# Chunked retention with transposes by DMA, and a second matmul in seven products, in a fused retention and hard-swish MLP kernel

## The chip, the cores and the metric

The kernel runs on one core of a Trainium2 chip. The metric is the device time of one launch in microseconds. Each kernel was run several times; medians with their lowest and highest run are given. A run's own record also has its span (first to last instruction in the trace) and the mean clock that the tensor engine was granted, as a share of full speed.

The engines are named as the profile names them: PE is the tensor engine (PEld its weight loads), DVE the vector engine, ACT the scalar engine, POOL is GpSimd, SP is the engine that here only issues DMA. A `q` behind a name (ACTq, SPq) means the sequencer of that engine, for instance while it issues a DMA.

## The reference

```python
# q, k, v: (8 batches, 8 heads, 576 positions, 64), float32
scores = q @ k^T / sqrt(64)
gamma  = 1 - 2.0 ** (-5 - h)                        # one decay per head
ret    = scores * where(i >= j, gamma ** (i - j), 0)
x      = (ret @ v)  as (8 * 576 tokens, 8 * 64)      # 4608 x 512
h      = x @ w_in                                    # 512 -> 2048
g      = h * clip(h + 3, 0, 6) / 6
out    = g @ w_out                                   # 2048 -> 512, float32
```

## The kernel before

Both kernels compute in fp16 with fp32 sums in PSUM. The kernel before handles one batch (576 tokens) of retention at a time, two heads together. It loads q, k and v through GpSimd's casting DMA queue, transposes q and k on PE, computes all 576 x 576 scores of the causal half, multiplies them by a table of decays on DVE, and multiplies by v. Between these steps it emits units of the MLP for blocks of 512 tokens that are ready.

```python
for b in range(B):
    # ... token blocks whose batches are done are queued; pop_units(4)
    for c in range(H // 2):                          # two heads
        # ... cast_load of q, k, v on the gpsimd queue
        for nix, nat in enumerate((qn16, kn16)):
            pst = psum.tile([P, S], FP16, tag="pp")
            for j in range(NCH):                     # 5 chunks: 4 x 128 + 64
                nc.tensor.transpose(pst[:, P*j:P*j+sj], nat[0:sj, j, :], ident16[...])
            # copy to SBUF: q by vector, k by scalar
        pop_units(2)
        for grp in bgrp:                             # 4 groups of score columns
            # ... matmuls kt2 x qt2 into pms[0], pms[1]
            for h2 in range(2):
                nc.vector.tensor_tensor(out=at16s[h2][...], in0=pms[h2][...],
                                        in1=dmask[...], op=ALU.mult)     # L210
        pop_units(2)
        for (s0, s1) in m2sc:
            # ... matmuls vn16 x at16s, scalar.copy into xt16              # L230, L236

def moe_unit(kb, kind, ix):                          # block of 512 tokens
    if kind == 0:                                    # "up": one of 16
        for dmc in range(NCC):                       # 4 matmuls of 512 columns, L122
            nc.tensor.matmul(ph, win16[:, dmc, ...], xt16[:, dmc, tok0:tok0+MBLK], ...)
        nc.scalar.activation(u, ph, ACTF.Relu, bias=0.5, scale=1/6)         # L126
        nc.vector.scalar_tensor_tensor(out=gt16[:, fc, :], in0=u, scalar=1.0,
                                       in1=ph, op0=ALU.min, op1=ALU.mult)   # L128
    else:                                            # "down": one of 4
        for fc in range(NFC):                        # 16 matmuls of 512 columns, L136
            nc.tensor.matmul(pout, gt16[:, fc, P*mc:P*mc+P], wout16[:, fc, :], ...)
        # ... scalar.copy to osb, store
```

## Time and profile before

| | before |
|---|---|
| time, first three runs | 454.21 us median (450.7 to 455.75) |
| span of the profiled run | 448.7 us |
| PE busy | 394.0 us, 88% |
| first up-projection matmul | at 47.8 us |
| period of one batch in the middle | 48.4 us, PE busy 44.2 us of it |
| one block's up, one block's down, alone | 13.8 us each |

The first lines are from the profile's page: the span, the busy time of each engine, the busy share of the engine in 40 equal slices (a digit is tenths), the granted clock in the same slices, and the chain of waits, which is the path followed back from the last instruction.

```profile
span 448.7 us, 6207 instructions
...
PE 394.0 (88%) x2368; PEld 181.7 (40%) x2368; DVE 230.5 (51%) x432; ACT 201.6 (45%) x349; POOL 177.6 (40%) x222
...
PE   0387999989998999899998999899989999899996
...
PEclk9999999999998999999999999999998999999999
...
PE 69%; DVE 18%; ACT 9%; issue 2%; POOL 1%; DVEq 0%; POOLq 0%
```

PE is busy in nearly every slice, at or near full clock. The kernel is bound by PE with short interruptions. The next lines are the end of the chain of waits in order of time (start, duration, what), where nothing but the MLP runs.

```profile
390.36 13.06 PE ph L122 x60
403.41 13.81 PE pout L136 x64
417.23 13.81 PE ph L122 x64
431.04 13.83 PE pout L136 x64
```

This gives the price of the MLP: 64 matmuls of 512 columns take 13.81 us, or 216 ns each. A batch period in the middle holds one up and one down, 27.6 us, so the other 20.8 us of the 48.4 us go to retention and its waits. The table of windows shows such periods (start:end, length, then busy time of each engine).

```profile
98.40:146.80 48.40, 44.45 (x277) 20.40 (x275) 27.21 (x52) 21.04 (x39) 20.74 (x24) 0.96 0.70 63
146.80:195.20 48.40, 44.22 (x282) 20.73 (x281) 27.21 (x52) 21.73 (x40) 20.79 (x24) 1.00 0.70 63
195.20:243.60 48.40, 44.22 (x282) 20.75 (x281) 27.21 (x52) 21.72 (x40) 20.80 (x24) 1.00 0.70 63
```

### The profile page before, as it was taken

What the parts mean: (1) busy time and instruction counts of PE and PEld (TensorE: products, weight loads), DVE (VectorE), ACT (ScalarE), POOL (GpSimd) and SP (SyncE); (2) the same over time, 40 slices, a digit from 0 to 9 for tenths busy, and PEclk for the clock granted to TensorE, in tenths of its full rate; (3) what the DMA queues carried; (4) which work ended last, traced back from release to release, by engine and by line L of the source; (5) the groups of instructions that cost most, each with busy time, mean ns of one, the idle gap of its engine ahead of it and who ended that gap; (6) DMA issues with size and microseconds to landing.
All of it is one profiled execution on the core that took longest, in us unless ns stands there. A gap on an engine that the chain in (4) does not pass through costs nothing.

```text
span 448.7 us, 6207 instructions
## 1 busy us (share of the span) xinstructions
PE 394.0 (88%) x2368; PEld 181.7 (40%) x2368; DVE 230.5 (51%) x432; ACT 201.6 (45%) x349; POOL 177.6 (40%) x222
## 2 busy tenths in 40 slices
PE   0387999989998999899998999899989999899996
PEld 0133444434443444444443444344443444344442
DVE  0254675347716672467635771667245763480540
ACT  5623564156522663356415652266325641571641
POOL 9966799763534444155326353445200000000000
PEclk9999999999998999999999999999998999999999
DMA  5999999985777766487568568776210001001101
GB/s 36 123 189 192 120 96 96 154 75 37 46 92 88 46 45 61 86 55 50 37 101 74 39 44 93 87 50 42 39 70 1 0 1 70 26 0 48 47 23 70
DMA packets 134700, 29.73 MB, mean 66 GB/s; under 512 B 126480, under 2 KB 130064, under 8 KB 134672
## 3 DMA queue, kind: packets, MB, share of 16 engines
q0 software_dynamic: 129488, 19.91, 60.8%
q1 hardware_dynamic: 5184, 9.44, 5.7%
q8 instruction: 18, 0.29, 0.3%
q14 instruction: 10, 0.08, 0.1%
HBM read 39.80 MB, written 9.44 MB: 110 GB/s over the span
## 4 chain that ended last, share of the span: by engine, by line
PE 69%; DVE 18%; ACT 9%; issue 2%; POOL 1%; DVEq 0%; POOLq 0%
PE pout L136 28%; PE ph L122 22%; DVE at16a L210 8%; DVE at16b L210 6%; PE pst L174 5%; ACT dmask L80 3%; ACT xt_104 L236 2%; ACT u L126 2%; ACT sb L180 2%; DVE gt_6_3580 L128 1%; DVE gt_5_3055 L128 1%; DVE gt_0_430 L128 1%; DVE gt_4_2530 L128 1%; DVE gt_3_2005 L128 1%; DVE gt_2_1480 L128 1%
## 5 line engine op out<-in xcount | busy, mean ns | idle before, releaser
L122 PE MATMUL ph<-xt_104,win_102 128*128 128x512 f16 x576 | 143.2, 383 | 5.7 <-DVE gt_1_955 L128 0.8
L126 ACT ACTIVATE u<-ph,cb 128x512 f32<-128x512 f32 x144 | 97.2, 687 | 53.2 <-PE ph L122 51.0
L122 PEld LDWEIGHTS <-win_102 128*128 128x128 f16 x576 | 52.6, 97 | 71.0 <-issue 19.5
L140 ACT COPY osb<-pout 128x512 f32<-128x512 f32 x36 | 21.1, 585 | 111.5 <-PE pout L136 111.5
L178 DVE COPY sb<-pst 128x576 f16<-128x576 f16 x32 | 14.5, 455 | 43.3 <-PE pst L174 43.3
L200 PEld LDWEIGHTS <-sb 64*128 64x128 f16 (+1 forms) x384 | 14.9, 100 | 42.5 <-ACT sb L180 18.2
L180 ACT COPY sb<-pst 128x576 f16<-128x576 f16 x32 | 20.4, 637 | 3.6 <-PE pst L174 1.6
L128 DVE SCALAR_TENSOR_TENSOR gt_8_4320<-u,ph 128x512 f16<-128x512 f32 x16 | 11.0, 688 | 16.6 <-ACT u L126 16.6
L128 DVE SCALAR_TENSOR_TENSOR gt_6_3580<-u,ph 128x512 f16<-128x512 f32 x16 | 10.7, 681 | 9.0 <-ACT u L126 8.9
L128 DVE SCALAR_TENSOR_TENSOR gt_2_1480<-u,ph 128x512 f16<-128x512 f32 x16 | 10.5, 679 | 9.2 <-ACT u L126 9.2
L128 DVE SCALAR_TENSOR_TENSOR gt_5_3055<-u,ph 128x512 f16<-128x512 f32 x16 | 10.7, 681 | 8.0 <-ACT u L126 7.8
L128 DVE SCALAR_TENSOR_TENSOR gt_4_2530<-u,ph 128x512 f16<-128x512 f32 x16 | 10.7, 681 | 8.0 <-ACT u L126 7.8
L128 DVE SCALAR_TENSOR_TENSOR gt_0_430<-u,ph 128x512 f16<-128x512 f32 x16 | 10.5, 680 | 8.3 <-ACT u L126 8.3
L128 DVE SCALAR_TENSOR_TENSOR gt_1_955<-u,ph 128x512 f16<-128x512 f32 x16 | 10.5, 680 | 8.1 <-ACT u L126 8.1
L128 DVE SCALAR_TENSOR_TENSOR gt_3_2005<-u,ph 128x512 f16<-128x512 f32 x16 | 10.5, 680 | 8.1 <-ACT u L126 8.1
L136 PE MATMUL pout<-wout_103,gt_2_1480 128*128 128x512 f16 x64 | 14.3, 379 | 0.2 <-DVE at16a L210 0.2
L136 PE MATMUL pout<-wout_103,gt_4_2530 128*128 128x512 f16 x64 | 14.3, 379 | 0.2 <-DVE at16a L210 0.2
L136 PE MATMUL pout<-wout_103,gt_0_430 128*128 128x512 f16 x64 | 14.3, 379 | 0.2 <-DVE at16a L210 0.2
L136 PE MATMUL pout<-wout_103,gt_1_955 128*128 128x512 f16 x64 | 14.3, 379 | 0.2 <-DVE at16a L210 0.2
L136 PE MATMUL pout<-wout_103,gt_5_3055 128*128 128x512 f16 x64 | 14.3, 379 | 0.2 <-DVE at16a L210 0.2
L136 PE MATMUL pout<-wout_103,gt_6_3580 128*128 128x512 f16 x64 | 14.3, 379 | 0.2 <-DVE at16a L210 0.2
L136 PE MATMUL pout<-wout_103,gt_3_2005 128*128 128x512 f16 x64 | 14.3, 379 | 0.2 <-DVE at16a L210 0.2
(1059 smaller groups left out, 775.9 us busy)
## 6 DMA issues: line engine op xcount, KB each, us to landing
out_dram<-osb SPq DMA_DIRECT2D x36, 256.0 KB, 2.0
win_102<-in_moe_w_in_dram POOLq DMA_DIRECT2D x2, 640.0 KB, 8.8
wout_103<-in_moe_w_out_dram POOLq DMA_DIRECT2D x2, 640.0 KB, 10.0
win_102<-in_moe_w_in_dram POOLq DMA_DIRECT2D x1, 768.0 KB, 9.9
wout_103<-in_moe_w_out_dram POOLq DMA_DIRECT2D x1, 768.0 KB, 10.5
qn_108<-in_q_dram POOLq DMA_DIRECT2D x2, 80.0 KB, 3.0
kn_109<-in_k_dram POOLq DMA_DIRECT2D x2, 80.0 KB, 3.0
vn_110<-in_v_dram POOLq DMA_DIRECT2D x2, 80.0 KB, 3.1
```

What stands on the lines that cost most here:

```text
L80: nc.scalar.activation(dmask[:, h, :], rsel, ACTF.Exp, bias=cb[:, 1:2], scale=float(np.log(gamma[h])))
L122: nc.tensor.matmul(ph, win16[:, dmc, P * fc:P * fc + P], xt16[:, dmc, tok0:tok0 + MBLK], start=(dmc == 0), stop=(dmc == NCC - 1))
L126: nc.scalar.activation(u, ph, ACTF.Relu, bias=cb[:, 0:1], scale=1.0 / 6.0)
L128: nc.vector.scalar_tensor_tensor(out=gt16[:, fc, :], in0=u, scalar=1.0, in1=ph, op0=ALU.min, op1=ALU.mult)
L136: nc.tensor.matmul(pout, gt16[:, fc, P * mc:P * mc + P], wout16[:, fc, :], start=(fc == 0), stop=(fc == NFC - 1))
L140: nc.scalar.copy(osb, pout)
L174: nc.tensor.transpose(pst[:, P * j:P * j + sj], nat[0:sj, j, :], ident16[0:sj, 0:sj])
L178: nc.vector.tensor_copy(sb, pst)
L180: nc.scalar.copy(sb, pst)
L200: nc.tensor.matmul(pms[h2][0:mt, co:co + ns], kt2[base:base + D, P * tcix:P * tcix + mt], qt2[base:base + D, a:bb], start=True, stop=True)
L210: nc.vector.tensor_tensor(out=at16s[h2][0:mtg, alo:alo + wid], in0=pms[h2][0:mtg, 0:wid], in1=dmask[0:mtg, 2 * c + h2, alo:alo + wid], op= ...
L236: nc.scalar.copy(xt16[h2 * D:h2 * D + D, c, b * S + s0:b * S + s1], pos[h2][h2 * D:h2 * D + D, 0:s1 - s0])
```

## The change

The intent is to make retention linear in the length of the sequence and to take its transposes off PE.

- **Chunks.** A batch's 512 first positions are four chunks of 128. q is multiplied by gamma^(i-e) and k and v by gamma^((e-j)/2) each, so a chunk's scores need only a 0/1 mask, and the sum of k^T v stays in PSUM as a state without being decayed. A chunk takes 24 matmuls of 128 columns: 8 for the scores, 8 for the values, 4 with the state of earlier chunks, 4 that add to the state.
- **Tails.** The 64 last positions of two batches make one more chunk, and the tails of all eight batches form a ninth token block. There are 36 chunks.
- **Transposes by DMA.** q and k of a chunk (256 KB) are transposed from SBUF to SBUF by one DMA, issued by ACT.
- **Seven products.** The down-projection of eight blocks is done as a 2 x 2 block product with seven products of 16 matmuls of 256 columns; DVE builds the sums. It runs one block behind the up-projection.
- **Order by hand.** No scheduler moves instructions: each engine runs what it is given in the order of the program. The preparation of a chunk is `load` (three DMAs on SP, six for a tail), `cast` (three multiplications on GpSimd), `xpose` (the transpose, ACT). Its use is `ret1` (scores and mask) and, some matmul groups later, `ret2` (the rest). How far preparation runs ahead of use is set in `advance`, called at the end of each `ret2`.

```diff
-            for nix, nat in enumerate((qn16, kn16)):
-                ...
-                    nc.tensor.transpose(pst[:, P * j:P * j + sj],
-                                        nat[0:sj, j, :], ident16[0:sj, 0:sj])
+    def cast(c, engs):
+        ...     # qk16[q|k] = staged q, k times table; vpad = staged v times table
+    def xpose(c):
+        qk = qk16s[c]
+        qt = work.tile([P, 8, P], FP16, tag="qkT", bufs=4, name="qkT")
+        qkTs[c] = qt
+        nc.scalar.dma_start_transpose(qt, qk.rearrange("p a h d -> p (a h d)"))
+    def ret1(c):
+        ...     # sc = kT x qT, 8 matmuls (L140); at = sc * mask on vector (L147)
+    def ret2(c):
+        ...     # xp = v x at + state x qT (L162, L167); state += k x v (L184)
+        ...     # xt <- xp on scalar (L189), s16 <- state on scalar (L196)
+    ...
+    nxt = [4]
+    nxp = [5]
+    def advance(i):
+        while nxp[0] < NCHK and nxp[0] <= i + 2 and nxp[0] < ncast[0]:
+            xpose(order[nxp[0]])
+            nxp[0] += 1
+        if nload[0] < NCHK and nload[0] <= i + 7:
+            load(order[nload[0]])
+            nload[0] += 1
+        if ncast[0] < nload[0] and ncast[0] <= i + 3:
+            cast(order[ncast[0]], G3)
+            ncast[0] += 1
+    def r2():
+        if nxt[0] < NCHK:
+            ret2(order[nxt[0]])
+            advance(nxt[0])
+            nxt[0] += 1
+    xpose(order[5])          # six chunks are cast and transposed by here
+    nxp[0] = 6
+    ...                      # blocks 0 and 1: up() with r1(), r2() between
+    for mc in range(4):
+        r1()
+        down_plain(0, mc)    # 16 matmuls of 512 columns, L248
+        r2()
+        tbuild(mc)
+    for kb in range(2, 9):
+        ...                  # 16 up(kb, fc), with r1() at 2, 9 and r2() at 5, 12
+        product(pb, "P1")    # pb = kb - 1; 16 matmuls of 256 columns, L312
+        r1()
+        product(pb, "P6")
+        r2()
+        product(pb, "P2")
+        r1()
+        product(pb, "P7")
+        r2()
+        ...                  # P5, r1, P4, r2, P3
```

## The prediction

> **What bounds the kernel now.** The tensor engine, in program order. The page gives PE 88% busy of a 448.7 us span (VectorE 51%, ScalarE 45%, GpSimd 40%); the chain of waits is 69% PE, 18% VectorE, 9% ScalarE. In time it shows about 50 us before the first up-projection matmul, seven batch periods of 48.4 us, and 54.5 us of two token blocks alone. There one up-projection of a block (64 matmuls, 128x512) takes 13.8 us and one down-projection 13.8 us (216 ns a matmul). So a batch period is 27.7 us of MLP and about 20.7 us of retention, of which some 4 us per period is the chain sitting in the VectorE mask products (0.60 to 0.69 us each).
>
> **What the change does.**
> - Removes all PE transposes (0.82 us per head pair) with their PSUM copies, and the quadratic part: a head pair now streams 2x1600 columns twice. Chunked, a 128-token chunk of all heads needs 24 matmuls of 128 columns. Transposes in the trace start about 90 ns apart, and 64-row pairs start together, so I estimate 1.7 us a chunk, 7.7 us a batch (4.5 chunks) against 20.7.
> - Seven products of 16 matmuls of 256 columns replace 64 of 512 for eight blocks: 112 x about 110 ns = 12.3 us against 13.8 (estimate). Gain 12 us in all.
> - VectorE: mask work falls from about 16 us to 5.5 us a batch; the sums for the seven products and five PSUM additions add about 8.5 us. ScalarE: relu stays (16 x 0.69 us a block), plus 36 DMA transposes issued from it; nothing in this trace shows their issue time, I assume about 2 us each.
> - Input loads move from GpSimd's casting queue to SP, in the same 256-byte rows. GpSimd multiplies instead; the Trainium skill ("GPSIMD Engine Reference", Performance versus the Vector engine) has 4.5 us for a 2048-element two-input fp32 operation, so I estimate 1.1 us per 512 and 3.5 us a chunk, below the 7 us a chunk is due in.
> - DMA: the windows show the 16 queues full at about 110 GB/s written as fp16, i.e. 220 GB/s read, while q, k, v are loaded. 28.3 MB at that rate is 129 us, weights and output some 50 us, and the transposes (256 KB each) about 1 us each at the 261 GB/s of "DMA: Bandwidth & Descriptors", Latency and other measured facts. About 215 us of the span: not the bound, except in the first 60 us.
>
> **Sum (span).** Head until the first up-projection: 26 us (loads, casts, four serial chunks), plus 5 us waiting for loads of chunks six to eight. Then PE: nine up-projections 124, one plain down 14, eight seven-product downs 98, 32 chunks 54: 290 us. Small stalls 12 us (ScalarE and PE are nearly equal in the up stage, about 17.5 us each), tail 4 us. Together 337 us; before's timed runs exceed its profile span by 5.5 us. **Prediction 343 us, 8 in 10 between 312 and 388.** Faster by over 2%: 0.95; within: 0.03; slower: 0.02.
>
> **What would show it.** First up-projection matmul near 26 us; period of a block in the middle 34 to 37 us; product matmuls 110 ns apart; PE at or above 85% after the head; chain mostly PE; VectorE about 26 us and ScalarE below 30 us per block.
>
> **What would make it wrong.** DMA transposes that occupy ScalarE or the queues much longer than 2 us, delaying relu and so PE's four PSUM buffers; loads slower than 220 GB/s, so that chunks arrive late and PE waits (GpSimd multiplies would then wait on DMA); 128-column matmuls nearer 60 ns (about 15 us better).

## The result, and the profile after

| | before | after |
|---|---|---|
| time | 452.45 us median of 4 runs (450.3 to 455.8) | 431.12 us median of 4 runs (426.88 to 436.98) |
| span of the profiled run | 448.7 us | 431.8 us |
| PE busy | 394.0 us | 318.7 us |
| PE idle | 54.7 us | 113.1 us |
| mean granted clock | 0.991 | 0.919 |
| first up-projection matmul | 47.8 us | 35.15 us |

The ratio of the times is 0.9448, 95% interval 0.9349 to 0.9547. Ratios here are the mean time of one kernel's fast runs over that of the other's fast runs of the same rounds, so they are not quite the ratio of the medians. Two of the four runs after, the profiled one among them, are marked slow because they are over 1.5% above the fastest; the fast ones had clocks of 0.932 and 0.923, so the low clock is no property of the slow runs. Their median is 427.8 us, which is the number to compare other fast runs with. The first experiment below has a profile with the same picture.

The kernel became faster, but by 21 us by these medians (25 us by the ratio of the fast runs) where 111 us were predicted. PE lost 75 us of busy time and gained 58 us of idle time. The page of the kernel after:

```profile
span 431.8 us, 6156 instructions
...
PE 318.7 (74%) x2368; PEld 197.1 (46%) x2368; DVE 228.1 (53%) x323; ACT 154.3 (36%) x273; POOL 110.0 (25%) x115
...
PE   0435966618754488877896869786979999999983
...
PEclk9999986959668878999989899998799999999999
DMA  9999983499256639777957597779533102020123
...
q1 hardware_dynamic: 126336, 46.15, 52.5%
q10 hardware_dynamic: 38016, 9.44, 14.8%
...
PE 50%; DMA 36%; SPq 5%; DVE 4%; ACT 2%; issue 1%; POOL 1%; POOLq 0%; ACTq 0%
```

DMA has 36% of the chain of waits, yet after the first 60 us the DMA row is full in a few slices only. This suggests that the chain waits for the duration of single transfers more than for the capacity of the queues; the experiments below test it. The list of waits (engine, line and tile, what it waited for: us in total, times, longest) and the view of the tile `qkT`, the transposed chunk, name the transfer:

```profile
PE sc L140 <- DMA qkT<-qk: 94.8, 29, 12.6
...
L131 ACTq DMA_TRANSPOSE qkT<-qk x36: 1247/1302/2072, 6.4 to 335.8; - x36
...
DMA to landing us min/median/max: 3.0/4.9/10.8
```

For 29 of 36 chunks, PE stood idle until the transpose of exactly this chunk had landed, for 94.8 of its 113.1 idle us (12.6 us of them for the very first chunk, 77.7 us after the first up-projection). Issuing one costs ACT's sequencer 1.3 us (median), and it lands 4.9 us after issue (median). The chain in order of time, in the stretch of the plain down-projection of block 0:

```profile
117.47 6.16 DMA qkT<-qk
...
123.67 0.61 PE sc L140 x8
124.28 6.07 PE po L248 x16
...
131.35 6.11 DMA qkT<-qk
...
137.50 0.61 PE sc L140 x8
138.11 5.98 PE po L248 x16
```

This reads: a transpose is issued, PE waits 6 us for it, computes the scores, runs one down group; then the rest of the chunk, and only now is the next transpose issued. The same stretch as a timeline (start, duration, engine and line, what, and in brackets the idle time before with its end):

```profile
117.13 0.36 SPq L240 DMA_DIRECT2D out_dram<-osb  x1
117.19 0.60 ACT L189 ACTIVATE xt<-xp 128x512 f16<-128x512 f32 x1
117.47 1.56 ACTq L131 DMA_TRANSPOSE qkT<-qk  x1
...
123.67 0.61 PE L140 MATMUL sc<-qkT 64*128 64x128 f16 x8 [6.30 <-DMA qkT<-qk]
```

Putting together, for single chunks, the end of GpSimd's last multiplication that the transpose needs, its issue, its landing and its use (all from the trace, us) shows that the input was ready long before:

```
chunk   input ready   issued   landed   scores start   PE idle before
 11         97.2       117.5    123.6      123.7            6.3
 12        102.6       131.3    137.5      137.5            6.3
 13        110.5       144.9    150.6      150.6            5.6
 20        188.2       208.8    214.0      214.0            1.9
 24        221.9       243.2    250.3      250.3            2.9
 30        270.3       293.8    300.7      300.8            3.6
```

The input was ready about 18 to 34 us before the transpose was issued, for every chunk from 11 on. ACT was not busy with other work all this time (36% over the span); the instruction simply stands late in its program.

The program says why. `advance(i)` runs after `ret2(i)`. Its bound for transposes reads `nxp <= i + 2`, two chunks ahead. But a transpose also needs `nxp < ncast`, and `ncast` is 6 when the first call comes, with `i = 4`, and rises by one per call because the cast is an `if`, and it stands after the transposes. So `ncast` is always `i + 2` when the transposes are looked at, and only chunk `i + 1` passes, the one that the very next `ret1` needs. The text says two ahead, the program does one.

The waits also cost a second time. The windows (length, busy PE, PEld, DVE, ACT, POOL, clock, DMA share, GB/s) show the clock that PE was granted:

```profile
64.00:106.00 42.00, 23.54 (x139) 11.54 (x140) 16.67 (x24) 15.64 (x25) 12.47 (x12) 0.76 0.85 156
106.00:158.00 52.00, 30.68 (x160) 13.64 (x158) 14.32 (x19) 7.82 (x16) 12.75 (x12) 0.74 0.48 89
...
238.00:282.00 44.00, 34.89 (x303) 23.13 (x304) 25.46 (x35) 16.63 (x29) 18.27 (x16) 0.96 0.82 144
```

Where PE idles 5.6 to 6.3 us between groups the mean clock is 0.74, and a down group of 16 matmuls takes 6.0 to 6.3 us; the same group of the kernel before took 3.45 us. A mean over such a stretch hides what happens in it. Here is one down group by itself, and the wait after it:

```profile
122.80:129.20 6.40, 5.53 (x20) 2.15 (x21) 2.45 (x3) 0.00 (x0) 2.08 (x2) 0.50 0.17 22
129.40:136.20 6.80, 1.85 (x21) 1.20 (x19) 0.00 (x0) 1.80 (x4) 1.04 (x1) 1.00 0.72 155
```

The clock is 0.50 while the group runs and 1.00 while PE mostly waits: it follows the work with a delay, so that nearly all of the group runs at half clock. The Trainium skill ("TensorE: Matmul & The Clock Gate", Part 1: The HAM clock gate) says that PE's clock is halved after an idle window of about 3.4 us and restored after a busy one; the 0.50 behind gaps of about 6 us agrees with it. A block's period in the steady part is 42 to 43 us (the score matmuls of chunks 18, 23, 28 and 33 start at 195.8, 238.3, 281.4 and 324.5 us), where 34 to 37 us were predicted.

### The profile page after: what moved, and what is told of

It is laid out like the page before. It is cut to its first block, busy times and chain, and to the rows that moved or that the text cites. A ratio compares the mean times of both kernels' runs of the same rounds, so it can differ in the third digit from the quotient of the medians.

```text
span 431.8 us, 6156 instructions
## 1 busy us (share of the span) xinstructions
PE 318.7 (74%) x2368; PEld 197.1 (46%) x2368; DVE 228.1 (53%) x323; ACT 154.3 (36%) x273; POOL 110.0 (25%) x115
## 3 DMA queue, kind: packets, MB, share of 16 engines
q1 hardware_dynamic: 126336, 46.15, 52.5%
q10 hardware_dynamic: 38016, 9.44, 14.8%
HBM read 36.70 MB, written 9.44 MB: 107 GB/s over the span
## 4 chain that ended last, share of the span: by engine, by line
PE 50%; DMA 36%; SPq 5%; DVE 4%; ACT 2%; issue 1%; POOL 1%; POOLq 0%; ACTq 0%
DMA qkT<-qk 30%; PE ph L218 20%; PE accB L312 10%; PE po L248 6%; SPq L94 4%; PE accA L312 4%; PE accC L312 4%; DMA st<-in_v_dram 3%; PE xp L162 3%; PE sc L140 3%; DMA st<-in_q_dram 2%; DVE g L223 2%; DMA wst<-in_moe_w_in_dram 1%; PE xp L167 1%; DVE ss L276 1%
## 5 line engine op out<-in xcount | busy, mean ns | idle before, releaser
L221 ACT ACTIVATE u<-ph,half 128x512 f32<-128x512 f32 x144 | 96.3, 687 | 108.5 <-PE ph L218 90.4
L218 PE MATMUL ph<-xt,win 128*128 128x512 f16 x512 | 132.0, 414 | 2.1 <-ACT xt L189 1.6
L223 DVE SCALAR_TENSOR_TENSOR g<-u,ph 128x512 f16<-128x512 f32 x144 | 95.5, 684 | 64.6 <-ACT u L221 63.5
L218 PEld LDWEIGHTS <-win 128*128 128x128 f16 x576 | 57.7, 104 | 72.9 <-issue 20.4
L140 PE MATMUL sc<-qkT 64*128 64x128 f16 x288 | 17.0, 248 | 94.8 <-DMA qkT<-qk 94.8
L117 POOL TENSOR_TENSOR qk<-st,tq 128x512 f16<-128x512 f32 x32 | 35.5, 1110 | 180.1 <-DMA st<-in_q_dram 114.5
L147 DVE TENSOR_TENSOR at<-sc,mask 128x1024 f16<-128x1024 f32 x32 | 39.1, 1223 | 69.1 <-PE sc L140 69.1
L312 PEld LDWEIGHTS <-ss 128*128 128x128 f16 x512 | 49.0, 98 | 8.0 <-DVE ss L276 1.7
L121 POOL TENSOR_TENSOR vpad<-st,tkv 128x512 f16<-128x512 f32 x36 | 38.8, 1078 | 22.3 <-DMA st<-in_v_dram 20.4
L312 PEld LDWEIGHTS <-g 128*128 128x128 f16 x384 | 37.7, 100 | 6.9
L117 POOL TENSOR_TENSOR qk<-st,tkv 128x512 f16<-128x512 f32 x32 | 34.7, 1084 | 5.5 <-DMA st<-in_k_dram 5.0
L162 PEld LDWEIGHTS <-vpad 128*128 128x128 f16 x288 | 23.8, 105 | 15.5 <-issue 11.8
```

The lines of the kernel that those rows point to most:

```text
L117: engs[ix].tensor_tensor(out=qk[:, ix, :, :], in0=st[:, ix, :, :], in1=tab.unsqueeze(2).to_broadcast([P, H, D]), op=ALU.mult)
L121: engs[ix].tensor_tensor(out=vp[:, :, 0:4:3, :], in0=st[:, ix, :, :].rearrange("p (a z) d -> p a z d", z=2), in1=tab.rearrange("p (a z) -> ...
L140: nc.tensor.matmul(sc[:, z, p, :], qt[z * D:z * D + D, HP + p, :], qt[z * D:z * D + D, p, :], start=True, stop=True)
L147: nc.vector.tensor_tensor(out=at.rearrange("p z a i -> p (z a) i"), in0=sc.rearrange("p z a i -> p (z a) i"), in1=m[:, :].unsqueeze(1).to_ ...
L162: nc.tensor.matmul(xp[:, p, :], vp[:, p, 2 * z:2 * z + 2, :], at[:, z, p, :], start=first, stop=False, skip_group_check=True)
L218: nc.tensor.matmul(ph, win16[:, m, P * fc:P * fc + P], xt[:, m, :], start=(m == 0), stop=(m == NCC - 1))
```

## Experiments

Two theories stood at the start. **Order**: the transposes are issued one chunk ahead, so their latency is on PE's path. **Bandwidth**: the queues are loaded with small packets of q, k and v, so the transposes, which share them, land late whenever they are issued. A third candidate was the stall of SP: the loads of output weights wait for buffers from about 47 to 82 us, and the load of chunk 9 stands behind them, which gave the longest single wait in mid kernel, 12.4 us. All ratios below are against the kernel before, in the same rounds on the same chip.

### x1_loads_early

```diff
-        if nload[0] < NCHK and nload[0] <= i + 7:
+        while nload[0] < NCHK and nload[0] <= i + 7:
```

> Loads of later chunks are issued up to the seven that the rule allows instead of one per step, so that they stand ahead of the output-weight loads on SP; transposes stay one chunk ahead. Theory A (the changed kernel loses its time because each DMA transpose is issued only one chunk before its use, and ScalarE's queue holds it back although its input was ready some 20 us earlier): only the 12.4 us wait at chunk 9 and a little of the cold clock go; 410 to 425 us. Theory B (the DMA queues as a whole are the bound, loads and transposes together): no gain, 425 to 435 us. A theory that late loads, not late transposes, are the cause would give under 380 us.

Measured: 429.9 us median (425.86 to 430.72, four runs), ratio 0.9481 (0.9398 to 0.9565). PE's waits for transposes were 82.7 us in 27 waits, landing after 4.7 us (median), clock 0.922. The wait at chunk 9 shrank from 12.4 to 7.0 us, and the time stayed where it was: PE now waited 8.0 us for casts of output weights, for which it did not wait before. So the stall of SP is not the main cause. The time lies in the range expected under theory B, bandwidth (425 to 435 us), and outside that under theory A, order (410 to 425 us): a miss of the theory that x2 then bears out. This run shows the waits of the kernel after: 83.4 us of idle time after the first up-projection, 65.1 us of it waits for transposes.

### x2_ahead2

x1, and one word more:

```diff
-        if ncast[0] < nload[0] and ncast[0] <= i + 3:
+        while ncast[0] < nload[0] and ncast[0] <= i + 3:
```

Now `ncast` can reach `i + 4` in `advance(i)`, and the bound `i + 2` of the transposes takes effect. With this word alone, without that of x1, the build stops with a deadlock, so that kernel was not run; the reading, not traced, is that a cast then waits for a load that SP, in order, cannot reach. That is why x1 is the base, and why x1 was measured by itself.

> As x1_loads_early, and multiplies are emitted while they may, so that each transpose is issued two chunks ahead instead of one. Theory A: the wait of the score matmuls for the transposed tile falls from 95 us to below 35 us (what is left is in the head), the granted clock rises from 0.92 to above 0.96, time 350 to 375 us. Theory B (DMA queues are the bound): that wait stays above 65 us and the time above 400 us.

Measured: 364.28 us (363.62 to 366.01, four runs), ratio 0.8055 (0.7993 to 0.8118). One word took away 65.6 us against x1. It makes the casts earlier too, but in x1 as in the kernel after the input of every chunk from 11 on lay ready over 17 us before the issue, so it acts through the earlier issue. The granted clock came out at 0.959 to 0.966, about the 0.96 expected. The waits for transposes and their landing, from the list of waits and the tile view of x2_ahead2:

```profile
PE sc L140 <- DMA qkT<-qk: 27.5, 7, 12.6
...
DMA to landing us min/median/max: 3.0/5.8/10.0
```

A transpose took longer to land than in the kernel after (5.8 against 4.9 us), while the same DMA traffic fell into less time. Yet the waits fell from 94.8 to 27.5 us, and in the trace none is left after chunk 13. Chunk 20, for example, was issued at 161.3, landed at 167.4 and was used at 172.7 us. The windows of x2_ahead2 show three blocks' periods in a row:

```profile
178.00:211.00 33.00, 32.92 (x295) 22.05 (x293) 24.65 (x35) 17.23 (x32) 18.11 (x17) 1.00 1.10 195
211.00:244.00 33.00, 32.41 (x292) 21.54 (x291) 24.70 (x35) 16.39 (x29) 14.61 (x14) 1.00 0.84 147
244.00:277.00 33.00, 32.96 (x296) 22.09 (x295) 25.60 (x38) 16.94 (x30) 6.90 (x6) 1.00 0.29 65
```

PE is full at full clock, and a block takes 33.0 us, slightly less than the 34 to 37 us predicted. The chain in order of time in the first of these windows gives the prices of the new work:

```profile
184.94 0.22 PE state L184 x4
185.16 1.75 PE accA L312 x16
186.91 0.33 PE sc L140 x8
187.24 1.85 PE accB L312 x16
```

A product of 16 matmuls takes 1.75 to 1.85 us, and a chunk takes 0.33 us for its scores, about 0.67 us for values and state terms and 0.22 us to add to the state, 1.22 us in all, or 51 ns a matmul.

### x3_ahead3

x1, with the bounds one further:

```diff
-        while nxp[0] < NCHK and nxp[0] <= i + 2 and nxp[0] < ncast[0]:
+        while nxp[0] < NCHK and nxp[0] <= i + 3 and nxp[0] < ncast[0]:
-        if ncast[0] < nload[0] and ncast[0] <= i + 3:
+        while ncast[0] < nload[0] and ncast[0] <= i + 4:
```

> As x2_ahead2 with transposes three chunks ahead. Theory A: a transpose lands 3 to 9 us after issue and a step of a chunk takes 5 to 9 us, so two ahead hides nearly all; three ahead gives 0 to 8 us more than x2_ahead2. Theory B: same as the changed kernel, above 400 us.

Measured: 360.55 us (359.38 to 366.27, five runs of which one slow), ratio 0.7943 (0.7852 to 0.8033). Waits for transposes were 27.1 us in 5 waits. The second step ahead gave nearly all of the gain. The third gave 4.2 us by the medians of the fast runs (360.0 against 364.3), which the overlapping intervals do not separate from nothing. The steady period is again 33.0 us with PE full, so what is left lies in the first part, before block 2, save for some 8 us of idle time in the tail.

### x4_ahead2_plain

x2, with the plain down-projection for all blocks. The sums, the seven products and the tables of weight differences are gone:

```diff
-        product(pb, "P1")
-        ...
-        product(pb, "P3")
+        for mc in range(4):
+            r1()
+            down_plain(pb, mc)
+            r2()
```

> x2_ahead2 with the plain second matmul (64 of 512 columns) for every block in place of the seven products. If PE is the bound once the transposes are early (theory A), it is 8 to 14 us slower than x2_ahead2 (16 products matmuls of 256 columns at about 110 ns, seven times, against 64 at 216 ns, eight blocks, 12 us). If DMA is the bound (theory B), within 3 us of x2_ahead2.

Measured: 373.09 us (371.56 to 373.93, four runs), ratio 0.824 (0.8176 to 0.8304). The seven products are worth 8.8 us, of the 12 us predicted. PE's busy time differs by 12.7 us (310.6 against 297.9), so the products themselves do what was said, and about 4 us of it are given back as idle time elsewhere. The seven products are at most 3 us of why the change fell short.

### x5_noload

The kernel after, without the loads of q, k and v from the seventh chunk on. Six constant staging tiles are reused as they are. **The result is wrong** (relative error 1.32).

```diff
-        st = work.tile([P, 3, H, D], FP32, tag="st", bufs=6, name="st")
+        n = nst[0]
+        nst[0] += 1
+        st = sts[n % 6]                 # six constant tiles
         stage[c] = st
+        if n >= 6:
+            return
```

> The changed kernel, transposes still one chunk ahead, but q, k and v are loaded for the first six chunks only and later chunks reuse those six staging tiles; the result is wrong on purpose. Some 23 of 28 MB of loads go. If a transpose is late only because of its own latency (issue to landing 4.9 us median, 3.0 us in the stretches with little load traffic), landing falls to about 3.1 us, the wait of the score matmuls from 95 to 45 to 65 us, time 385 to 410 us: still far above the kernel with transposes two ahead (364), which loads everything. If the load traffic were the cause, the wait should nearly vanish and the time fall to 364 us or less.

Measured: 374.44 us (371.34 to 376.86, four runs), ratio 0.8282 (0.8188 to 0.8376), clock 0.971. From the list of waits and the tile view of x5_noload (the lines of the program have moved by seven):

```profile
PE sc L147 <- DMA qkT<-qk: 52.7, 21, 13.1
...
DMA to landing us min/median/max: 3.0/3.2/10.9
```

The time came out below the 385 to 410 us that were expected of it, so the loads weigh more than the order theory allowed. The waits were within the expected 45 to 65 us; what the expectation left out is that PE's busy time would fall too, from 318.7 to 299.3 us, with the clock up from 0.919 to 0.971. With the loads gone most transposes land in 3.2 us, close to the minimum, and this nearly fits between issue and use. So neither theory holds in its pure form: the latency of a transpose was never under 3.0 us here, it was 4.9 us in the median with the loads and 3.2 us without most of them, and late issue exposes both parts.

### x6_ahead3_noload

x3, with the loads removed in the same way. **The result is wrong**, as in x5.

> x3_ahead3 with the same removal of loads (wrong result on purpose). From about 145 us on x3_ahead3 already runs at 33 us a block with PE full, so only the first 145 us can gain. If these are held by the DMA queues, 15 to 30 us go (330 to 345 us); if by the serial chunk chain and weight casts, under 8 us.

Measured: 341.46 us (340.77 to 343.76, four runs), ratio 0.756 (0.7502 to 0.7619), clock 0.990, waits 22.2 us in 6 waits, 19.7 us of it for the first five chunks. The time is within the 330 to 345 us expected if DMA holds the first part, and the first product starts 21.5 us earlier than in x3 (123.2 against 144.7 us). Together with the others this makes a square (medians of the fast runs, us):

| | with loads | without loads | the loads are worth |
|---|---|---|---|
| one chunk ahead | 427.8 (after) | 374.4 (x5) | 53.4 |
| three chunks ahead | 360.0 (x3) | 341.5 (x6) | 18.5 |
| the order is worth | 67.8 | 32.9 | |

The two gains overlap: together they are 86.3 us, while 67.8 and 53.4 would add up to 121.2. Order alone recovers 67.8 us with all loads in place; the loads cost 53.4 us where each delay falls on PE, and 18.5 us where a chunk's lead hides it. Taking either away removes much of the same waiting, so the waits have two causes, and the order is the larger one. (x3 has the word of x1 too, which by itself made no difference clear of the noise: 429.9 against 427.8 us.) The 341.5 us of x6 come within 2 us of the 343 us predicted, which is a coincidence: the prediction had the loads in.

### x7_order

x6 said that 18.5 us still hang on the loads, in the first part. In x2 PE sat idle 13.9 us there before down groups of block 0, until output weights had been cast (9.0 us for a cast on DVE, 4.9 us for one on ACT). x7 puts the first loads into another order: the kernel after with the cast `while`, the input weights between the chunks, and the last output weights requested later, so that SP does not stop at them.

```diff
-    for i in range(6):
-        wload(0, i)
+    for i in range(2):
+        wload(0, i)
     load(order[4])
+    for i in range(2, 5):
+        wload(0, i)
     load(order[5])
-    wload(0, 6)
-    wload(0, 7)
+    for i in range(5, 8):
+        wload(0, i)
 ...
-        if ncast[0] < nload[0] and ncast[0] <= i + 3:
+        while ncast[0] < nload[0] and ncast[0] <= i + 3:
 ...
-            for i in range(6):
+            for i in range(4):
                 wload(1, i)
 ...
-            if i < 2:
-                wload(1, 6 + i)
+            if i < 4:
+                wload(1, 4 + i)
```

> Right result. Transposes two chunks ahead, loads one per step as in the changed kernel, and the order of the first loads changed: weights of the first up-projection between the chunks, chunks five and six later, only four output-weight loads queued at once (no block of SP). If the head is a matter of what stands first in the DMA queue, 3 to 12 us better than x2_ahead2 (352 to 361 us); if of its total bytes, within 3 us of it.

Measured: 353.52 us (352.38 to 355.9, four runs), ratio 0.7825 (0.7763 to 0.7887). The result is correct. It is 10.8 us better than x2 by the medians, and the best of all kernels run with a correct result: 22% below the kernel before, 17% below the kernel after. In the traces PE's waits for output weights fell from 13.9 us to 5.1 us, and those for transposes after the first up-projection from 10.5 to 7.9 us. The edit changes the order of the input weights, that of two chunks and the number of output-weight loads asked for at once; the run does not tell these apart. The first product of the seven starts at 133.3 us, against 146.8 us in x2. The page of x7_order:

```profile
span 351.7 us, 6148 instructions
...
PE 295.0 (84%) x2368; PEld 189.4 (54%) x2368; DVE 229.9 (65%) x323; ACT 154.4 (44%) x273; POOL 112.3 (32%) x115
...
PE   0344857778499899999999989999999999999891
...
DMA  9999999999889997999599949994400300300313
```

PE is full from the twelfth slice on; before it, the DMA row is at 9 or 8 in every slice. Here, in the first 100 us, the queues are full.

### x8_order_ahead3

x7, with transposes three ahead (`i + 3`, cast `i + 4`), as in x3.

> Right result. x7_order with the transposes three chunks ahead. In x7_order some transposes of the first 110 us still land just before their use (waits of 0.3 to 5.6 us there, about 9 us in all besides the first), so 0 to 8 us better than x7_order (345 to 354 us) if these are a matter of issue order; no change if the transposes there are late because their loads are, which the issue times close behind the multiplies in that stretch suggest.

Measured, on another chip: 354.96 us (353.86 to 357.53, four runs), ratio 0.7853 (0.7785 to 0.7921). There is no gain over x7; the intervals overlap for the most part. The time is the second of the outcomes foreseen above, but the trace bears out its reason (late loads) only in part. Chunks 7 to 12 do land well before use now, 6.5 to 20 us. There was little left to gain: PE's waits for transposes after the first up-projection went from 7.9 to 6.6 us, and the one long wait, at chunk 6, stayed (5.6 and 5.9 us), its input ready at 45.5 and 45.3 us and issued 2.8 us later in both. PE's waits for the mask rose from 8.9 to 13.6 us. What would shorten the first part further was not tried and stays open.

## Why the prediction was wrong

The direction was right, with 0.95 on faster, and the time was outside the range: 431 us against 343 (312 to 388). Set beside the span after, term by term (us):

| term | predicted | after | x3_ahead3 |
|---|---|---|---|
| until the first up-projection | 26 | 35.1 | 36.7 |
| PE busy after it | 290 | 308.9 | 289.3 |
| PE idle after it (loads 5, stalls 12, tail 4) | 21 | 87.7 | 35.7 |
| span | 337 | 431.8 | 361.8 |

- **The step that failed is "Small stalls 12 us".** In the kernel after, PE's idle time behind the head is 87.7 us against the 21 us of the whole term, and 77.7 us of it are waits for transposes. The prediction gave the small stalls to ACT and PE being nearly equal in the up stage, and its sum has no time at all in which PE waits for a transpose; that holds only if transposes run far enough ahead of their use, as the bound `i + 2` seems to say. The cast counter holds them to `i + 1`, and x2 shows by one word that this was worth 65.6 us, clock included. x5 adds that the loads beside the transposes lengthen these waits (94.8 us with them, 52.7 us without most of them). The paragraph on what would make the prediction wrong named transposes that occupy ACT or the queues for over 2 us and so delay relu; their issue took 1.3 us. The issue was cheap; the place of it in the order, and the latency behind it, were not asked about.
- **The latency of a transpose was taken as its bandwidth.** The prediction used an estimate of 1 us for 256 KB, from a bandwidth of 261 GB/s, and never a time from issue to landing. That time is 3.0 us at least and 4.9 us in the median. A latency matters only where it is exposed: in x2 it was 5.8 us in the median and cost nothing after chunk 13.
- **PE's busy time grew by 19 us through the clock.** The sum charged every matmul at the full clock. The idle gaps lowered the granted clock, to 0.74 in the worst stretch; with the gaps gone (x3, same instructions) the term is 289.3 us, almost the 290 predicted. That agreement hides two errors: a chunk takes 1.22 us and not 1.7 us (32 chunks: 39 us, not 54), and part of the remaining time is still spent below full clock in the first part (0.79 in x3 from 82 to 112 us; x6, with a mean clock of 0.990, has 284.5 us in this term).
- **"DMA: about 215 us of the span" was too low.** The two queues q1 and q10 took 52.5% and 14.8% of the 16 engines' time over 431.8 us, 290 us in all, 64 us of it transposes (1.8 us each, not 1). These are sums over packets, whose times can overlap: the same sum over x3 from 112 to 145 us gives 1.25 of the 16 engines, so 290 us is no lower bound of the time. DMA is not the bound in the kernel after, but the reserve was thin: in x3 the DMA row stays at 8 or 9 until about 235 us, and removing the loads gives 18.5 us even there.
- **The head was 9 us longer.** The first four chunks' transposes took 5.9 to 10.8 us to land beside full queues, and the chunks follow each other in series. That is not all of it: in x7 they took 5.9 to 7.4 us, and the head was still 34.2 us. What else the head needs was not tested.
- **The step from span to time.** The 5.5 us added to the span compared a median with the span of one run; the profiled run after took 1.7 us more than its own span (433.49 against 431.8).
- **What was right.** The period of a block with PE full: 33.0 us (34 to 37 predicted). The seven products: 109 to 116 ns a matmul (110 predicted), 8.8 us of a predicted 12 in x4 against x2. GpSimd's multiplication: 1.08 to 1.11 us per 512 (1.1 estimated from the Trainium skill, "GPSIMD Engine Reference", Performance versus the Vector engine). The mask: 1.22 us a chunk, 5.5 us a batch, as predicted. DVE 24 to 26 us and ACT 16 to 17 us a block (x2), within the bounds named.

What is not settled is how the 70 us of span between the profiled runs of the kernel after and x3 divide between waiting and clock in a strict sense, since each gap causes some of the slow clock behind it. In the traces, PE idle fell by 50 us and PE busy by 20 us.

## What to carry to other kernels

When a program fixes its order by hand, follow its counters through two or three calls and write down, for one unit of work, when it is issued and when it is used; the bound in the text is not the distance that the program keeps, if another counter holds it back. Cost a transfer by two numbers, its share of the queues and its time from issue to landing, and let the second decide how far ahead it must be issued. Here, gaps of about 6 us on the tensor engine cost more than their length: the 16 matmuls behind each ran at a lower clock, 6.0 to 6.3 us against 3.45.

## What the Trainium skill lacked or had wrong

- "DMA: Bandwidth & Descriptors", Latency and other measured facts, gives a DMA transpose a bandwidth only (261 GB/s, by estimate 1.0 us for 256 KB). Here a 256 KB transpose from SBUF to SBUF took 3.0 us from issue to landing at least, 4.9 us in the median and 10.8 us at most beside loads of small packets, and 1.3 us of the issuing sequencer's time (1.25 to 2.07 us). Elsewhere the skill has 1309 ns for a DMA transpose of 128 x 128 ("VectorE: DVE Perf Modes", The three transpose paths) and a fixed part of about 2.0 us for a DMA on GpSimd's path (the first page, Anatomy of one DMA), but no time from issue to landing for a transpose of this size issued by ACT, and for the issue only cycles of earlier generations for other shapes (the first page, in its part on trn3).
- "Advanced Engine Details and Errata", X-Bar Transpose, calls transposes as fast as regular DMAs. Here the packets of the queue of transposes took 64 us of all 16 engines for 36 of 256 KB, 1.8 us each, or about 148 GB/s (9.44 MB in 64 us), below the 261 GB/s of the other page and the 350 to 400 GB/s of this one. With most loads removed (x6) it was still 53 us (15.5% of 339.4 us), about 179 GB/s, where the queue of the other transfers in the same run had about 272 GB/s (22.55 MB in 24.4%). Packet times can overlap, so the comparison of the two queues is safer than the figures themselves.
- "TensorE: Matmul & The Clock Gate", Back-to-back issue gap, has streams of weight loads and matmuls at about 81 ns for 128 columns and 131 ns for 512, and calls its formula N / 2.4 + 2.5 ns fit for isolated matmuls only. Here, with a weight load for each matmul, streams ran at 216 ns for 512 columns (64 in 13.81 us) and 109 ns for 256 (16 in 1.75 us), and the four that add to the state at 55 ns for 128 (0.22 us), which are the formula's numbers, and for 128 and 512 columns those that Part 1 of the same page measured for back-to-back matmuls.
